# A 480-byte tile at the right end of on-chip memory in a fused window-attention and two-layer MoE kernel

## The chip, the cores and the metric

The kernel runs on one core of a Trainium2 chip (trn2). The metric is device microseconds of one execution, lower is better. Engines: PE is TensorE (matmuls; PEld its weight loads), DVE is VectorE, ACT is ScalarE, POOL is GpSimd, SP is SyncE, which issues the DMAs.

## The reference

Three blocks follow one another, all in float32, on 1536 tokens of width 512.

```
x = window_attention(q, k, v)           # (2, 8, 768, 64): 16-wide window, plus 24 block summaries
x = relu(x @ w_in) ** 2 @ w_out         # 512 -> 2048 -> 512; weights come as float64
rms = sqrt(mean(x * x, -1) + 1e-6); xn = x / rms * rms_g
g = xn @ w_gate; val = xn @ w_val       # 512 -> 1536
out = (silu(g) * val) @ w_out2          # 1536 -> 512
```

## The kernel before

**Work and order.** Attention runs over 12 groups of 128 tokens (`group`, `ptrans`, `av`) with plain float32 matmuls; its results go, split in a high and a low part, into `xhi`/`xlo`. Weights arrive as float64 words, are turned to float32 (`conv_a`, `conv_b`) and split in a high and a low part of type float32r (`split`, lines 195 and 196), which together fill one 4096-byte slot, the tile that `wslot` hands out. A product of the MoE layers is three float32r matmuls: high by high, high by low, low by high (`mm3`, line 509; `ff_out`, line 530). The first layer's `wi0` to `wi3` and `wo0` to `wo3` run between the attention groups, on halves of 256 columns. After attention everything is done in rounds (`steps_of`): for a few units f, for each of the 3 chunks of 512 tokens, `product` with 12 matmuls of 512 columns and, two steps later, `ff_out` with 12 more. In `product` (tiles `h`, `g`, `v`) the weights are the operand that is loaded into the array, and the tokens stream; in `ff_out` (tiles `y`, `z`) the hidden values are loaded and the weights stream, 512 columns of 4 bytes, 2048 bytes of each partition. The program is put in order by the tile framework's scheduler.

**Where tiles lie.** Every partition of on-chip memory is filled from both ends. Pools on the left hold `ident`, the raw and converted weights (`wpool`, 14 slots at 20,480 + 4096 n bytes), `xhi`/`xlo`, the hidden values `hhi`/`hlo` (their last tile ends at byte 174,080) and most partial sums `yp`. Pools with `side="right"` are laid downwards from byte 229,344, which is 32 more than a multiple of 64. During attention that is `ap`: `kT`, `vx`, `ksum`, `qT`, `t`, `vm`, `pT` and four 32-byte tiles `mx`, `sm`. When attention is over, `ap` is closed and `w2pool` takes its place: 9 more weight slots, at 192,480 + 4096 n bytes, and `grow`, `yp10`, `yp11`. Sizes on the right are multiples of 64 bytes, but for `mx` and `sm` (32 each), so nearly every tile there starts 32 bytes past a multiple of 64; every weight slot on the left starts at a multiple of 64.

**Which weights lie where.** Once `w2pool` is open, `wslot` counts the converted units: of each 18 the first 9 go to the right, the next 9 to the left.

```
k = side["n"] % (NRIGHT + NW - RAWS)     # 9 + 14 - 5 = 18
side["n"] += 1
if k < NRIGHT:
    return side["pool"].tile([P, 2, DM], F32R, tag="w2", name=name, bufs=NRIGHT)
```

In the order in which units are converted (`order`), this gives:

| side | units |
|---|---|
| left | wi0-4, wo0-3 (before `w2pool`); wi10-14, wo8-11; wg2-4, wv2, wv3, wp0-3; wg8-10, wv8-10, wp6-8 |
| right | wi5-9, wi15; wo4-7, wo12-15; wg0, wg1, wg5-7, wg11; wv0, wv1, wv4-7, wv11; wp4, wp5, wp9-11 |

Right are 32 units, all of them used on 512 columns, each by 12 matmuls for each of 3 chunks.

Of the kernel before, what the change touches and what calls it, by code (L numbers as in the profile page):

```python
# [10 lines left out]
F32 = mybir.dt.float32  # L11
# [21 lines left out]
def tile_window_attention_moe_moe2(  # L33
# [16 lines left out]
    P = 128  # L50
# [33 lines left out]
    psY = ctx.enter_context(tc.tile_pool(name="psY", bufs=MT // 2, space=PSUM))  # L84
    psB = ctx.enter_context(tc.tile_pool(name="psB", bufs=1, space=PSUM))

    ident = cpool.tile([P, P], F32, name="ident")
    make_identity(nc, ident)
    um = cpool.tile([P, KW + QT], F32, name="um")
# [55 lines left out]
    side = {"n": 0, "pool": None}  # L145
# [713 lines left out]
```

## Time and profile before

| | |
|---|---|
| three runs | 680.22, 681.25 (median), 683.86 us |
| profiled execution | span 681.0 us from the first to the last instruction; no other time is given for it |
| PE busy | 654.7 us (96%), 3644 matmuls |
| DVE / ACT / POOL busy | 404.4 / 305.8 / 4.1 us |
| moved by DMA | 54.22 MB, mean 80 GB/s |

The profiled span lies 0.25 us below the median of the runs. Busy shares are means over stages that have different limits: attention with its many short steps takes the first 160 us or so, and the MoE layers the rest. The chain of waits follows the work that ended last back from the end; where it shows one engine with no wait between its pieces, the time of that stretch is the sum of that engine's instructions. A piece of the chain "x12" is 12 instructions of one line, and its length runs to the start of the next piece, so its length by 12 is what one instruction costs the stretch. The mean duration of one matmul in the grouped view is longer than that, since matmuls overlap.

### The profile page before, as it was taken

Reading aid. Unit: us, or ns where it says so; the run is one execution under the profiler, and the core shown is the slowest. Engines: PE = TensorE matmul, PEld = TensorE weight load, DVE = VectorE, ACT = ScalarE, POOL = GpSimd, SP = SyncE. Lnnn points to the kernel's source line nnn. Section 1 sums busy time; section 2 is a strip of 40 time slices with the busy share of each in tenths; the row PEclk is TensorE's granted clock in tenths of the full one; section 3 lists DMA queues with packets and bytes.
Section 4 is the critical chain, followed back from the end, with each engine's and each line's share of the span. In section 5 each row is a group of like instructions: output and inputs, shape, how many; then the busy total and the mean of one; then the engine's idle time right before and its main releaser. Section 6 shows DMA issues by size and latency. Waiting matters only on the chain.

```text
span 681.0 us, 9361 instructions
## 1 busy us (share of the span) xinstructions
PE 654.7 (96%) x3644; PEld 533.9 (78%) x3644; DVE 404.4 (59%) x733; ACT 305.8 (45%) x637; POOL 4.1 (1%) x25
## 2 busy tenths in 40 slices
PE   7768998999999999999999999999999999999997
PEld 5456957888888888888888888888888888888885
DVE  4799758656999579726574795189613171313132
ACT  4597558365866447326352773167411131111110
POOL 2000000000000000000000000000000000000000
PEclk9769998999999999999999999999999999999999
DMA  9678556222522223001021251015300000001011
GB/s 244 147 247 190 131 171 160 68 49 91 189 62 94 93 63 123 31 1 62 13 98 46 68 180 62 1 34 162 113 1 1 0 1 0 1 1 62 1 62 63
DMA packets 78188, 54.22 MB, mean 80 GB/s; under 512 B 46080, under 2 KB 72704, under 8 KB 78144
## 3 DMA queue, kind: packets, MB, share of 16 engines
q1 hardware_dynamic: 78144, 53.62, 26.7%
q8 instruction: 29, 0.48, 0.3%
q14 instruction: 15, 0.12, 0.1%
HBM read 50.07 MB, written 3.15 MB: 78 GB/s over the span
## 4 chain that ended last, share of the span: by engine, by line
PE 86%; SPq 5%; DVE 4%; DMA 2%; ACT 1%; issue 1%; DVEq 0%; ACTq 0%
PE y L530 19%; PE h L509 18%; PE g L509 15%; PE v L509 15%; PE z L530 14%; SPq L404 3%; PE xps L488 1%; PE pps L467 1%; PE s L418 1%; SPq L303 1%; DMA raw_wo<-in_moe_w_out_dram 1%; PE xps L500 1%; ACT t L447 1%; SPq L292 1%; DMA raw_wi<-in_moe_w_in_dram 1%
## 5 line engine op out<-in xcount | busy, mean ns | idle before, releaser
L509 PE MATMUL h<-xhi,w_wi 128*128 128x512 f32 (+1 forms) x480 | 136.6, 357 | 1.8 <-ACT xhi L478 1.2
L530 PE MATMUL y<-w_wo,hhi 128*128 128x512 f32 x384 | 120.7, 398 | 1.9 <-ACT hhi L520 1.7
L805 DVE TENSOR_TENSOR sg<-v,sg 128x512 f32<-128x512 f32 x36 | 24.9, 692 | 134.8 <-PE v L509 134.8
L509 PEld LDWEIGHTS h<-xhi,w_wi 128*128 128x128 f32 x480 | 87.3, 195 | 15.7 <-ACT xhi L478 1.9
L509 PE MATMUL v<-xhi,w_wv 128*128 128x512 f32 x288 | 95.6, 393 | 0.0
L509 PE MATMUL g<-xhi,w_wg 128*128 128x512 f32 x288 | 95.4, 393 | 0.0
L530 PE MATMUL z<-w_wp,hhiz 128*128 128x512 f32 x288 | 89.0, 392 | 0.0
L509 PE MATMUL h<-xlo,w_wi 128*128 128x512 f32 (+1 forms) x240 | 86.1, 359 | 1.8 <-DVE xlo L479 1.8
L530 PEld LDWEIGHTS y<-w_wo,hhi 128*128 128x128 f32 x384 | 72.4, 190 | 18.2 <-ACT hhi L520 1.9
L530 PE MATMUL y<-w_wo,hlo 128*128 128x512 f32 x192 | 75.1, 401 | 0.0
L803 ACT ACTIVATE sg<-g 128x512 f32<-128x512 f32 x36 | 21.6, 600 | 104.6 <-PE g L509 102.4
L509 PEld LDWEIGHTS v<-xhi,w_wv 128*128 128x128 f32 x288 | 54.0, 188 | 12.3
L509 PEld LDWEIGHTS g<-xhi,w_wg 128*128 128x128 f32 x288 | 54.0, 188 | 12.3
L530 PEld LDWEIGHTS z<-w_wp,hhiz 128*128 128x128 f32 x288 | 54.0, 188 | 11.9
L657 ACT ACTIVATE r<-h 128x512 f32<-128x512 f32 x48 | 28.7, 598 | 71.3 <-PE h L509 71.2
L509 PE MATMUL g<-xlo,w_wg 128*128 128x512 f32 x144 | 56.6, 393 | 0.0
L509 PE MATMUL v<-xlo,w_wv 128*128 128x512 f32 x144 | 56.5, 393 | 0.0
L530 PE MATMUL z<-w_wp,hloz 128*128 128x512 f32 x144 | 55.9, 392 | 0.0
L509 PEld LDWEIGHTS h<-xlo,w_wi 128*128 128x128 f32 x240 | 46.9, 195 | 9.0 <-DVE xlo L479 2.4
L658 DVE TENSOR_TENSOR r<-h,r 128x512 f32<-128x512 f32 x48 | 33.0, 687 | 35.0 <-ACT r L657 35.0
L520 ACT CAST hhiz<-sg 128x512 fp32r<-128x512 f32 x36 | 22.4, 621 | 69.7 <-DVE sg L805 69.4
L530 PEld LDWEIGHTS y<-w_wo,hlo 128*128 128x128 f32 x192 | 36.2, 191 | 8.1 <-issue 0.2
(125 smaller groups left out, 897.5 us busy)
## 6 DMA issues: line engine op xcount, KB each, us to landing
raw_wi<-in_moe_w_in_dram SPq DMA_DIRECT2D x16, 512.0 KB
raw_wo<-in_moe_w_out_dram SPq DMA_DIRECT2D x16, 512.0 KB
raw_wg<-in_moe_w_gate_dram SPq DMA_DIRECT2D x12, 512.0 KB
raw_wv<-in_moe_w_val_dram SPq DMA_DIRECT2D x12, 512.0 KB
raw_wp<-in_moe_w_out_dram SPq DMA_DIRECT2D x12, 512.0 KB
kr<-in_k_dram SPq DMA_DIRECT2D x12, 256.0 KB
qr<-in_q_dram SPq DMA_DIRECT2D x12, 256.0 KB
vr<-in_v_dram SPq DMA_DIRECT2D x6, 512.0 KB
```

The costliest lines, as they stand in the source:

```text
L292: nc.sync.dma_start(t.rearrange("p h e d -> p h (e d)"), src[b, :, 2 * P * c : 2 * P * (c + 1), :].rearrange("h (p e) d -> p h (e d)", e=2),)
L303: nc.sync.dma_start(t[:, j].rearrange("p (h d) -> p h d", h=H), src[b, :, o : o + P, :].rearrange("h p d -> p h d"),)
L404: nc.sync.dma_start(vx[j : j + n, i0 + u], v[b, :, o : o + n, :].rearrange("h s d -> s h d"))
L418: mark[("s", g)] = nc.tensor.matmul(sl[e][QT * u : QT * u + QT, p, :], qT[rr, p, QT * u : QT * u + QT], kT[rr, p, o : o + NK], start=True, ...
L447: mark[("exp", g)] = nc.scalar.activation(t[:, h], t[:, h], AF.Exp, bias=mx[:, h : h + 1], accum_out=sm[:, h : h + 1])
L509: nc.tensor.matmul(ps, a_, b_, start=(i == 0), stop=(i == tot - 1))
L520: nc.scalar.copy(hi[:, 0:n], s[:, 0:n])
L530: nc.tensor.matmul(y, a_[:, ms], b_, start=(first and i == 0), stop=(last and i == 2))
L657: nc.scalar.activation(t, ps, AF.Relu)
L658: nc.vector.tensor_tensor(t, ps, t, op=ALU.mult)
L803: nc.scalar.activation(t, psg, AF.Silu)
L805: nc.vector.tensor_tensor(t, psv, t, op=ALU.mult)
```

## The change

A pool `lpool` is opened on the right before any other pool there, and one tile of 120 float32 values for each partition, 480 bytes, is placed in it. Nothing writes or reads the tile. All pools opened later on the right lie 480 bytes lower: their top is byte 228,864 = 64 x 3576, the weight slots of `w2pool` lie at 192,000 + 4096 n, and every tile there starts at a multiple of 64 except two of the 32-byte tiles `mx`, `sm`. Tiles on the left stay where they were. No instruction, wait or DMA is added, taken away or moved on any engine. Line numbers after this place grow by 2.

```
     psB = ctx.enter_context(tc.tile_pool(name="psB", bufs=1, space=PSUM))
 
+    lpool = ctx.enter_context(tc.tile_pool(name="lpool", bufs=1, side="right"))
+    lpool.tile([P, 120], F32, name="edge")
     ident = cpool.tile([P, P], F32, name="ident")
```

## Rows read from the trace of the kernel before

**Rows 1.** The page: the span, busy time by engine, PE in 40 slices

```profile
span 681.0 us, 9361 instructions
...
PE 654.7 (96%) x3644; PEld 533.9 (78%) x3644; DVE 404.4 (59%) x733; ACT 305.8 (45%) x637; POOL 4.1 (1%) x25
...
PE   7768998999999999999999999999999999999997
```

**Rows 2.** Busy time in stretches: from:to, length, engines (instructions), clock, DMA share, GB/s

```profile
23.10:29.90 6.80, 4.34 (x24) 4.04 (x26) 4.99 (x13) 4.01 (x7) 0.00 (x0) 0.50 0.51 103
40.20:50.30 10.10, 6.84 (x32) 6.04 (x31) 9.68 (x20) 8.57 (x26) 0.00 (x0) 0.50 0.64 155
67.50:70.80 3.30, 3.30 (x17) 3.20 (x16) 3.30 (x5) 1.01 (x1) 0.00 (x0) 0.50 0.83 251
115.30:122.00 6.70, 6.70 (x54) 5.66 (x55) 4.97 (x9) 5.33 (x20) 0.00 (x0) 0.50 0.45 141
150.00:676.00 526.00, 525.54 (x2389) 429.38 (x2389) 294.10 (x534) 210.89 (x373) 0.00 (x0) 1.00 0.17 56
```

**Rows 3.** What PE waited for, whole span: us, times, longest

```profile
PE qps L364 <- DMA qr<-in_q_dram: 7.6, 2, 4.9
...
PE y L530 <- ACT hhi L520: 1.7, 1, 1.7
...
PE y L530 <- ACT w_wo L195: 0.2, 1, 0.2
```

**Rows 4.** The chain that ended last, one round of the second layer: start, us, piece

```profile
471.72 2.73 PE g L509 x12
474.45 2.79 PE v L509 x12
477.24 2.73 PE z L530 x12
479.97 2.80 PE g L509 x12
482.77 2.79 PE v L509 x12
485.56 2.73 PE z L530 x12
...
493.88 2.80 PE z L530 x12
```

**Rows 5.** The same chain: two pieces of 18 matmuls of `y`, first layer

```profile
186.00 4.20 PE y L530 x18
...
285.86 4.08 PE y L530 x18
```

**Rows 6.** The same chain: left weights right behind right ones, then left alone

```profile
571.86 2.75 PE g L509 x12
574.60 2.72 PE v L509 x12
577.32 2.72 PE z L530 x12
```

**Rows 7.** Instructions by line and shape: the casts into slots, and two attention matmuls

```profile
L488 PE MATMUL xps<-pT,vx 120*64 120x64 f32 x384 | 17.7, 234 | 0.1
L418 PE MATMUL s<-kT,qT 64*64 64x120 f32 x384 | 17.6, 278 | 0.0
...
L195 ACT CAST w_wo<-x_wo 128x512 fp32r<-128x512 f32 x16 | 9.9, 620 | 3.2 <-DVE x_wo L189 2.5 <-PE y L530 0.6
...
L195 ACT CAST w_wp<-x_wp 128x512 fp32r<-128x512 f32 x12 | 7.4, 618 | 3.2 <-PE v L509 2.0 <-PE z L530 0.7 <-DVE x_wp L189 0.6
```

**Rows 8.** Busy time in the stretch right after attention, columns as in rows 2

```profile
165.00:205.00 40.00, 40.00 (x186) 32.98 (x186) 39.01 (x75) 27.75 (x50) 0.00 (x0) 1.00 0.44 144
```

**Rows 9.** The whole chain's shares of the span, by line

```profile
by line: PE y L530 19.2%; PE h L509 18.2%; PE g L509 14.6%; PE v L509 14.6%; PE z L530 14.4%; SPq L404 2.8%; PE xps L488 1.4%; PE pps L467 1.2%; PE s L418 1.1%; SPq L303 1.0%; DMA raw_wo<-in_moe_w_out_dram 1.0%; PE xps L500 0.8%; ACT t L447
```

## The prediction

> **What bounds the kernel now.** I first read the page: PE is busy for 654.7 of 681.0 us, and the slices show it at 9 tenths from the eighth slice on [rows 1]. Then the stretches: between 150 and 676 us PE is busy for 525.54 of 526.00 us at a granted clock of 1.00, which is the 2.4 GHz level [rows 2], while its waits for the other engines' results in the MoE layers are small: 1.7 us for ACT's high part of a hidden tile, 0.2 us for a converted weight [rows 3]. So from 150 us on only the pace of the matmuls counts. Before that the kernel is a mixture of short waits (7.6 us for `qr` alone [rows 3]) and of four stretches at half the clock [rows 2]. The whole chain says the same by line: the five rows of lines 509 and 530 hold 81% of the span, and attention's PE rows for `xps` and `s` 1.4% and 1.1% [rows 9].
>
> The change moves no instruction, so the question is whether a matmul or another instruction cares where its tile begins. The kernel before answers part of that itself, because the same matmul is run on weights in left slots (a start at a multiple of 64) and in right slots (32 past one). In one round of the second layer [rows 4] the pieces of 12 matmuls are, by the list of units: `g` on wg4 (left) 2.73 us, `v` on wv4 (right) 2.79, `z` on wp2 (left) 2.73, wg5 and wv5 (right) 2.80 and 2.79, wp3 (left) 2.73, and, two pieces further on, wp4 (right) 2.80. The side decides, not the line: `z` takes 2.73 on wp2 and wp3 and 2.80 on wp4, and `g` takes 2.73 on wg4 and 2.80 on wg5. That holds whether the weights stream (`z`) or are loaded (`g`, `v`). The first layer agrees: 18 matmuls of `y` on right slots (wo4, wo5) take 4.20 us, 18 on left slots (wo10, wo11) 4.08 [rows 5]. Per matmul this is 4.20/18 = 233.3 ns against 4.08/18 = 226.7 ns: 6.67 ns more. At 2.4 GHz that is 16 cycles, and 16 columns of 4 bytes are 64 bytes, which looks like one more piece of 64 bytes to be fetched when a row that is itself whole pieces starts in the middle of one.
>
> **The sum.**
> - *The right-slot matmuls.* 32 units x 3 chunks x 12 matmuls = 1152, each 6.67 ns shorter: -7.7 us. All lie in the stretch where PE has no gaps, so all of it is on the path. This is the term that carries the forecast.
> - *Left pieces behind right ones.* A piece with loaded left weights that follows a right piece takes 2.75 us instead of 2.72 [rows 6] (there wg8 behind wp5, then wv8 and wp6 at 2.72). The chain has 19 such whole pieces at 2.75: 19 x 0.03 = -0.6 us. The pieces of 2.79 (last matmul at the left pace already) and of 2.73 (last one at the right pace) about cancel each other.
> - *Attention's matmuls.* `vx`, `kT`, `qT`, `t` and `pT` move as well. No row shows such a float32 matmul with its tile at another start, so I bound it. At the one end nothing: a loss I exclude, since `vx`, `qT` and `pT` come to the start that is the faster one in [rows 5], and the windows of `kT`, which begin at steps of 304 bytes, only exchange one set of starts for another when all move by 480. At the other end each of the 384 + 384 instructions of `xps` and `s` [rows 7] saves the same 6.67 ns; two always run side by side, so 768 x 6.67 / 2 = 2.6 us. I take -0.3, near the lower end: half of the 768 work on `kT`, and an `xps` takes 234 ns for 64 columns [rows 7] where the big ones advance by 512 in 226.7, so one more piece has more time to come in beside it.
> - *VectorE and ScalarE.* They write the slots and read the tiles on the right. The casts into slots take 620 ns for `w_wo`, 8 of whose 16 units are right, and 618 ns for `w_wp`, 5 of 12 [rows 7]. A cost per right slot would pull the first above the second by 8/16 - 5/12 = 8% of it; a difference of 2 ns bounds it to about 25 ns a cast, on engines that wait for PE in the MoE layers. I put it at nothing; the cover is PE's unbroken work.
> - *DMAs.* 72 loads and 12 copies write `vx`. `vx` does not stand among PE's waits. I put them at nothing; what hides them is the work that PE does while `vx` is filled.
> - *What is late next.* Right after attention DVE is busy for 39.01 of 40 us [rows 8], since it converts the next weights there. If a faster PE had to wait for it, at most the gain of that stretch would be lost, about 9 right pieces x 0.08 = 0.7 us. Elsewhere nothing is close: between 150 and 676 us DVE is busy for 294 of 526 us [rows 2].
>
> Sum: -7.7 - 0.6 - 0.3 = -8.6 us, from the execution's 681.0 to 672.4 us. That execution lies 0.25 us below the median of the runs, so against the median of 681.25 I forecast 672.7 us, 1.3% faster.
>
> **A rule that speaks against it.** The rows show that 32 bytes past a multiple of 64 is a slow start for a right slot, or that the right side is slow whatever its start. The Trainium skill, in "SBUF — State Buffer", section "Specifications (TRN2)", gives cachelines of 16 bytes as the unit whose crossing costs something. Both 32 and 0 are multiples of 16, so by that rule the two starts touch equally many lines and the sum would be 0, a time of 681.25 us; the rows' step of 64 bytes' worth of columns does not fit it.
>
> **The rivals.**
> - *A: the side costs, not the start.* The right side could be slower because of where it lies (its addresses, or what it shares), and then moving it by 480 bytes changes nothing: 681.25 us. For it: before the change no right slot starts at a multiple of 64, so the trace cannot part the two. Against it: the hidden tiles that are loaded for the left `y` and `z` pieces reach up to byte 174,080 and go at 2.72 us, and the lowest right slot at 192,480 (wi5, wv4, wg11, wo12) is as slow as the highest, so a border would have to fall in just that gap; and a far address gives no reason for 16 cycles. Beside this stands the Trainium skill's rule of 16-byte lines, above, which would lead here.
> - *B: slower, through the clock.* In the first 150 us the clock falls to 0.50 (1.2 GHz) in four stretches, 3.3 to 10.1 us long and 26.9 us in all [rows 2]. A shift of attention's short waits could add one, if idle time of PE grows around the loads of `qr`. Price: a stretch like the longest, on work that PE bounds, costs 10.1/2 = 5 us; with A that gives 686 us. It decides the sign only if the gain in the MoE layers fails as well, or if over 17 us are added at half the clock. Against it: no instruction there changes its place or its number.
> - *C: only part.* PE gets its gain and gives 3 to 5 us of it back, by such a stretch of clock or by waits for conversions: 677 us. Against it: PE's gaps between 150 and 676 us sum to 0.46 us [rows 2], so the others keep up with it by a margin.
>
> **How the numbers follow.** Forecast 0.88, A 0.07, C 0.03, B 0.02. About 0.5%, 3.4 us, is what a measurement of this kernel can tell from no change; C's 677 lies beyond that. So faster 0.91, same 0.07, slower 0.02. The predicted time is the forecast's, 672.7. Its range: down by the rest of attention's bound (2.3 us, of which I take 1.7, since part of it lies beside other work), to 671.0; up by the terms that could fail (0.7 of DVE, 0.6 of the pieces behind right ones, 0.8 of attention and its DMAs) and by 1.2 us for the scatter of the runs, whose highest lay 2.6 above their median: 676.0. That holds nearly all of the forecast's 0.88, and needs no part of A.
>
> **What would show it.** Right: in the chain of the new profile every whole piece of 12 on line 511 (509 before) and on line 532 (530 before) takes 2.72 us, the same for units of both sides; 2.75 and 2.80 are gone; the stretch from the end of attention to the last matmul is some 8 us shorter, with PE busy throughout and DVE's and ACT's means as before. Wrong: pieces of 2.80 stay on right units (A); another stretch at clock 0.50 before 150 us (B); PE waits on `w_wi` or `w_wo` around 165 to 205 us (C).

## The result and the profile after

The changed kernel takes 674.5 us (median of 4 runs, 673.34 to 675.57), the one before 680.74 us (4 runs, 680.16 to 683.86): a ratio of 0.9899 with a 95% interval of 0.9868 to 0.9931, so it is faster by 0.7 to 1.3%. The forecast was 672.7 us, with a range of 671.0 to 676.0. The profiled execution of the changed kernel has a span of 673.9 us, against 681.0 before: 7.1 us less. With it comes its own time, 675.57 us, 1.7 us more than the span; in all executions on record a time is 1.7 to 1.9 us more than its span, so the sum is best compared span with span.

The chain of waits after, for the same stretch of the second layer as [rows 4]: start, length and piece.

```profile
468.19 2.72 PE g L511 x12
470.92 2.72 PE v L511 x12
473.63 2.72 PE z L532 x12
476.36 2.72 PE g L511 x12
479.07 2.72 PE v L511 x12
481.80 2.72 PE z L532 x12
...
489.95 2.72 PE z L532 x12
```

These are wg4, wv4, wp2, wg5, wv5, wp3 and wp4. Before, wv4, wg5, wv5 and wp4 stood at 2.79 or 2.80 and the left ones at 2.73; now no side can be told from the other.

To separate this from attention, the view by tile gives the last attention matmul (`xps`, last start) and the last matmul of all (`z`, last start). Before:

```profile
L488 PE MATMUL xps<-pT,vx x384: 222/222/368, 31.5 to 160.6; 120*64 120x64 f32 x192
...
L530 PE MATMUL z<-w_wp,hloz x144: 389/395/397, 393.8 to 676.2; 128*128 128x512 f32 x144
```

After:

```profile
L490 PE MATMUL xps<-pT,vx x384: 221/222/368, 32.6 to 161.5; 120*64 120x64 f32 x192
...
L532 PE MATMUL z<-w_wp,hloz x144: 388/390/398, 390.8 to 669.1; 128*128 128x512 f32 x144
```

From the end of attention to the last matmul it took 676.2 - 160.6 = 515.6 us, and takes 669.1 - 161.5 = 507.6 us: 8.0 us less. Attention itself ends 0.9 us later. The median duration of these `z` matmuls (the middle number) falls from 395 to 390 ns.

The stretches after, with the columns of [rows 2]:

```profile
24.80:31.60 6.80, 5.50 (x43) 5.20 (x44) 3.21 (x10) 3.42 (x7) 0.00 (x0) 0.50 0.48 91
41.80:52.10 10.30, 7.25 (x33) 6.85 (x33) 9.90 (x21) 8.78 (x25) 0.00 (x0) 0.50 0.63 142
113.50:123.80 10.30, 10.30 (x75) 8.47 (x75) 7.01 (x11) 6.75 (x22) 0.00 (x0) 0.50 0.48 137
150.00:669.00 519.00, 518.53 (x2397) 430.67 (x2396) 294.46 (x534) 211.16 (x375) 0.00 (x0) 1.00 0.17 56
165.00:205.00 40.00, 40.00 (x194) 33.76 (x193) 39.59 (x77) 28.42 (x51) 0.00 (x0) 1.00 0.45 145
```

Three stretches at half the clock in place of four, of about the same sum (27 us). From 150 us on PE has gaps of 0.47 us, as before. In the 40 us right after attention DVE is fuller still, 39.59 us [rows 8], and PE 40.00.

The instructions by line and shape that answer to [rows 7]:

```profile
L420 PE MATMUL s<-kT,qT 64*64 64x120 f32 x384 | 18.9, 291 | 0.0
L490 PE MATMUL xps<-pT,vx 120*64 120x64 f32 x384 | 17.7, 234 | 0.0
...
L197 ACT CAST w_wo<-x_wo 128x512 fp32r<-128x512 f32 x16 | 9.9, 620 | 3.2 <-DVE x_wo L191 2.7 <-PE y L532 0.5
...
L197 ACT CAST w_wp<-x_wp 128x512 fp32r<-128x512 f32 x12 | 7.4, 617 | 3.1 <-PE v L511 1.8 <-PE z L532 0.7 <-DVE x_wp L191 0.6
```

The casts and attention's `xps` take what they took. Attention's `s` is busy for 18.9 us instead of 17.6, but the median of one is 263 ns in both traces; the half-clock stretches lie at other places.

### The profile page after: what moved, and what is told of

It is laid out like the page before. It is cut to its first block, busy times and chain, and to the rows that moved or that the text cites. A ratio compares the mean times of both kernels' runs of the same rounds, so it can differ in the third digit from the quotient of the medians.

```text
span 673.9 us, 9361 instructions
## 1 busy us (share of the span) xinstructions
PE 646.7 (96%) x3644; PEld 534.0 (79%) x3644; DVE 403.7 (60%) x733; ACT 305.2 (45%) x637; POOL 4.0 (1%) x25
## 4 chain that ended last, share of the span: by engine, by line
PE 88%; SPq 4%; DVE 2%; DMA 2%; ACT 2%; issue 1%; DVEq 0%; ACTq 0%
PE y L532 19%; PE h L511 19%; PE v L511 15%; PE g L511 15%; PE z L532 14%; SPq L406 2%; PE xps L490 2%; PE s L420 2%; DMA raw_wi<-in_moe_w_in_dram 1%; PE pps L469 1%; SPq L305 1%; ACT t L449 1%; PE xps L502 1%; PE qps L366 1%; SPq L294 1%
## 5 line engine op out<-in xcount | busy, mean ns | idle before, releaser
L511 PE MATMUL h<-xhi,w_wi 128*128 128x512 f32 (+1 forms) x480 | 134.8, 354 | 2.5 <-ACT w_wi L197 1.7
```

Source lines behind the costliest of these rows:

```text
L511: nc.tensor.matmul(ps, a_, b_, start=(i == 0), stop=(i == tot - 1))
```

## The experiments

The first question was rival A: start or place. The second arose from the first answer: if the start counts, then why. "Mod 512" is what is left of a start address when whole multiples of 512 are taken off. "Stage" is the time from the last `xps` to the last matmul, from the rows by tile of each profile; it leaves out what attention's clock does.

| run | start of right slots (mod 512) | start of left operands (mod 512) | stage, us | ratio to before, 95% interval |
|---|---|---|---|---|
| before | 480 | 0 | 515.6 | |
| changed | 0 | 0 | 507.6 | 0.9899 (0.9868 to 0.9931) |
| e1_edge32 | 448 | 0 | 513.5 | 0.9986 (0.9961 to 1.0012) |
| e2_edge512 | 480 | 0 | 515.6 | 1.0002 (0.9981 to 1.0023) |
| e7_edge992 | 0 | 0 | 507.6 | 0.9861 (0.9793 to 0.9929) |
| e8_left480 | 480 | 480 | 507.6 | 0.9898 (0.9833 to 0.9962) |
| e5_left32 | 0 | 32 | 515.6 | one run |
| e10_edge224 | 256 | 0 | 507.6 | 0.9883 (0.9845 to 0.9921) |

**Start or place: 32 and 512 bytes.**

```
-    lpool.tile([P, 120], F32, name="edge")
+    lpool.tile([P, 8], F32, name="edge")       # e1_edge32
+    lpool.tile([P, 128], F32, name="edge")     # e2_edge512
```

> The tile at the right end is 32 bytes instead of 480, so everything on the right moves by 32 bytes only and starts at a multiple of 64, at addresses 32 below those of the kernel before. Theory (the start counts): as the changed kernel, about 674 us, and every piece of 12 matmuls with 512 columns at 2.72 us. Rival (the place on the right counts, and moving down by 480 took the tiles out of it): as the kernel before, about 681 us, with pieces of 2.80 on the right units.

> The tile at the right end is 512 bytes, so everything on the right lies 32 bytes lower than in the changed kernel and starts 32 past a multiple of 64 again. Theory (the start counts): as the kernel before, about 681 us, pieces of 2.80 us on the right units and 2.72 on the left ones. Rival (the place counts): as the changed kernel, about 674 us, all pieces at 2.72.

With 512 bytes, 32 below the changed kernel, the gain is gone: 681.13 us, a stage of 515.6 us. So 32 bytes up or down decide, not the region, and rival A falls. But with 32 bytes, where every tile starts at a multiple of 64 as well, the median is 680.02 us, no faster than before by its interval. The stage says what happened. The chain of e1_edge32:

```profile
465.58 2.72 PE g L511 x12
468.30 2.75 PE v L511 x12
471.05 2.72 PE z L532 x12
473.77 2.75 PE g L511 x12
...
487.48 2.80 PE z L532 x12
490.28 2.80 PE g L511 x12
```

`z` on wp4 (the piece at 487.48) still takes 2.80, that is, a streamed right slot at a multiple of 64 still costs 6.67 ns a matmul; loaded ones (wv4, wg5) cost 2.75, or 2.80 right behind a slow piece (wg7). A multiple of 64 is neither the condition nor enough. My theory and its rival are both wrong here.

**Other distances in one kernel.** The slot is made longer, and each unit starts at another place in it.

```
-                return side["pool"].tile([P, 2, DM], F32R, tag="w2", name=name, bufs=NRIGHT)
+                t = side["pool"].tile([P, 2 * DM + 16], F32R, tag="w2", name=name, bufs=NRIGHT)
+                o = (1, 0, 4, 12, 15, 8, 2, 6, 14)[k]
+                return t[:, o : o + 2 * DM].rearrange("p (e f) -> p e f", e=2)
```

> The changed kernel, but each right weight slot is 64 bytes longer and its unit starts at 4, 0, 16, 48, 60, 32, 8, 24 or 56 bytes into it, by its number among the right ones: four units (wi6, wi15, wg5, wv11) stay at 0, the other 28 lie off a multiple of 64. Theory (one more piece of 64 bytes, whatever the distance): every unit off 0 takes 2.80 us for 12 matmuls, those at 0 take 2.72; 28 x 36 x 6.67 ns = 6.7 us above the changed kernel, about 681 us. Rival 1 (only crossing lines of 16 bytes costs): 16, 32 and 48 at 2.72, the others slower. Rival 2 (the cost grows with the distance from 64): pieces between 2.72 and 2.80 in steps.

One execution took 680.24 us, with a stage of 514.5 us, near what "any distance costs" gives. But the units at 0 past a multiple of 64 were not fast (these slots, 4160 bytes apart, begin at different places within 512 bytes), and one at 16 past a multiple of 64 was:

```profile
472.75 2.80 PE v L513 x12
...
478.28 2.75 PE g L513 x12
481.03 2.72 PE v L513 x12
```

The `v` at 472.75 is wv4 (4 past a multiple of 64), the `g` at 478.28 wg5 (a multiple of 64, at 448 within 512), the `v` at 481.03 wv5 (16 past one, at 400 within 512). The slowest was a streamed unit, wo12 at 452 within 512: 2.86 us for 12 (the piece at 290.97), more than the 2.80 that one more piece of 64 bytes would give. None of the three theories fits that.

**Shorter rows.** In the kernel before, the streamed rows of `ff_out` are cut from 512 to 504 columns.

```
+                n = DM if first and i == 0 else DM - 8
                 nc.tensor.matmul(
-                    y, a_[:, ms], b_, start=(first and i == 0), stop=(last and i == 2)
+                    y[:, 0:n], a_[:, ms], b_[:, 0:n], start=(first and i == 0), stop=(last and i == 2)
                 )
```

> The kernel before (right slots 32 past a multiple of 64), but in the second product of both layers the streamed rows are 504 columns long, 2016 bytes, except in the first matmul of each sum: the last 8 columns get that one term alone. 2016 bytes touch 32 pieces of 64 bytes from a start at 0 and from a start at 32 alike. Theory (pieces are counted): pieces of 12 matmuls of y and z that stream from right slots are as fast as those from left slots, 2.68 to 2.72 us both, while h, g and v, where the weights are loaded, keep 2.80 against 2.72. Rival (a start at 32 costs 16 cycles whatever the length): y and z at 2.76 from the right and 2.68 from the left.

```profile
472.60 2.72 PE z L531 x12
475.32 2.80 PE g L509 x12
478.12 2.80 PE v L509 x12
480.92 2.72 PE z L531 x12
...
489.24 2.78 PE z L531 x12
...
497.62 2.76 PE z L531 x12
```

One execution took 678.03 us. Left units (wp2, wp3, at 472.60 and 480.92) are no faster for 8 columns less: 2.72, not 2.68, so here the number of columns alone does not set the pace; no run shows what does. Right ones take 2.76 (wp5, at 497.62), as the rival says, and 2.78 where the first matmul of every sum is a full one (wp4, at 489.24). They are not as fast as the left ones, which speaks against the theory, but the step is 0.04 us for 12 and not the rival's 0.08. Neither holds as a whole, and this run does not decide.

**Own start or start against each other.** In e7_edge992 the tile has 248 values, 992 bytes. In the other two runs a tile lies on the left, below the weight pool, on top of the kernel before (e8) and of the changed one (e5).

```
+    bpool = ctx.enter_context(tc.tile_pool(name="bpool", bufs=1))
+    bpool.tile([P, 120], F32, name="base")     # e8_left480; [P, 8] in e5_left32
     wpool = ctx.enter_context(tc.tile_pool(name="wpool", bufs=1))
```

> The tile at the right end is 992 bytes: the right side lies 512 bytes lower than in the changed kernel, and its weight slots start at a multiple of 512 again (not only of 64, as in the run with 32 bytes). Theory (what counts is the start within 512 bytes): all pieces of 12 at 2.72 us, a profiled span of about 674 us, some 7 us below the kernel before. Rival (the changed kernel lies at one lucky place): pieces of 2.75 to 2.80 us on right units and about 681 us.

> The kernel before, with the right side left where it was (its slots start at 480 past a multiple of 512), and a tile of 480 bytes put on the left below the weight pool, so that the left slots, the tokens and the hidden values start at 480 past a multiple of 512 too. Theory P (what counts is how the loaded and the streamed operand stand to each other): all pieces at 2.72 us, about 674 us, as the changed kernel, though no operand starts at a multiple of 64. Theory Q (each operand pays for its own start): all 2592 float32r matmuls pay, most of them for both operands; pieces of 2.80 to 2.88 us everywhere, 690 us or more.

> The changed kernel, with a tile of 32 bytes on the left below the weight pool: left weights, tokens and hidden values start at 32 past a multiple of 512, the right weights at 0. Theory P (the two operands' starts against each other): left units 2.72 us for 12 matmuls, as both operands lie at 32; right units 2.80; about 681 us. Theory Q (each pays for its own start): no piece at 2.72; right units 2.80, left units 2.80 or, if the two costs add, 2.88; about 690 to 700 us.

e8_left480 is the run that settles it. The right side stays as it was in the kernel before, 32 past a multiple of 64, and everything that meets it on PE is moved to the same distance. Now no float32r matmul has an operand at a multiple of 64, and all are fast: 674.75 us against 682.08 for the kernel before, a stage of 507.6 us. Its chain:

```profile
469.25 2.72 PE g L511 x12
471.97 2.72 PE v L511 x12
474.69 2.72 PE z L532 x12
...
491.01 2.72 PE z L532 x12
```

The `v` at 471.97 (wv4) and the `z` at 491.01 (wp4) are right units, the other two left ones.

e5_left32 is the counter-test: right slots where the change puts them, the left moved by 32 bytes. The whole gain is lost (a stage of 515.6 us), and in the chain the right units are the slow ones, though it is they that start at a multiple of 512:

```profile
472.88 2.73 PE g L513 x12
475.61 2.79 PE v L513 x12
478.40 2.73 PE z L534 x12
481.13 2.80 PE g L513 x12
...
495.04 2.80 PE z L534 x12
```

So theory P holds against Q: what costs is the distance between the starts of the loaded and of the streamed operand. Neither pays for its own start. Which two meet can be read in the trace of the kernel before, from the start of one matmul to the start of the next (the stretch of [rows 4]): the first eleven of wg4 (left) take 226 or 227 ns, the last, with wv4 (right) to be loaded next, 235; those of wv4 take 230 to 235, and the last, with a left operand next, 226. It is the streamed operand of one matmul against the loaded one of the matmul behind it. e7_edge992 gives the changed kernel's stage at another place: 671.88 us against 682.08.

**Which distances.** The slots 512 bytes longer, units at multiples of 64 (and 16, 32), then at finer steps; and the right side as a whole at 256.

```
+                t = side["pool"].tile([P, 2 * DM + 128], F32R, tag="w2", name=name, bufs=NRIGHT)
+                o = (64, 8, 16, 32, 48, 80, 96, 4, 112)[k]       # e6_scan
+                o = (36, 100, 28, 40, 20, 44, 52, 34, 60)[k]     # e9_scan2
```

> The changed kernel, but each right weight slot is 512 bytes longer and its unit starts at 256, 32, 64, 128, 192, 320, 384, 16 or 448 bytes past a multiple of 512, by its number among the right ones; tokens and hidden values stay at 0. Theory (period 512): every right unit is slower than 2.72 us for 12 matmuls, 2.80 for streamed weights and 2.74 to 2.80 for loaded ones; about 680 us. Rival (period 128 or 256): units at 256, or at 128, 256 and 384, take 2.72 like those at 0.

> The tile at the right end is 224 bytes, so that the right slots start at 256 past a multiple of 512, all other operands at a multiple of 512. Theory (the loaded and the streamed operand must start at the same place within 256 bytes): all pieces of 12 at 2.72 us; from the last attention matmul to the last of all 507.6 us, as in the changed kernel. Rival (within 512 bytes; that the units at 256 were fast was the luck of their neighbours): right pieces at 2.75 to 2.80 and up to 515.6 us.

> As the scan before, with the right units at 144, 400, 112, 160, 80, 176, 208, 136 and 240 past a multiple of 512. Theory in its plain form (any other distance within 256 bytes costs): no right piece at 2.72 us. Rival (the two reads meet only at some distances, and a loaded operand some 144 bytes off misses the streamed one): loaded units at 144 and 400 at 2.72 us, as the one unit at 400 in the first scan, streamed ones at 144 slow.

e6_scan and e9_scan2 were executed once each, 679.6 and 679.81 us. The chain of e6_scan: units at 256 (wv4, at 472.13), 32 (wg5), 64 (wv5), then 128 and 192 (wg6, wv6), 320 (wp4).

```profile
472.13 2.72 PE v L513 x12
474.85 2.73 PE z L534 x12
477.58 2.79 PE g L513 x12
480.37 2.80 PE v L513 x12
483.17 2.76 PE z L534 x12
485.92 2.79 PE g L513 x12
488.72 2.79 PE v L513 x12
491.51 2.75 PE z L534 x12
```

At 256 a loaded unit is as fast as at 0, and so is a streamed one (wo12, in the first layer, 2.73 with the next unit's first load in it). e10_edge224 confirms it for all right slots at once: stage 507.6 us, 672.6 us. The period is thus 256 bytes; 128 and 64 are not free. In e9_scan2 one more distance is fast in places:

```profile
291.48 2.80 PE y L534 x12
294.28 2.80 PE h L513 x12
297.08 2.77 PE y L534 x12
...
472.85 2.72 PE v L513 x12
...
478.29 2.73 PE g L513 x12
481.01 2.80 PE v L513 x12
483.81 2.77 PE z L534 x12
486.57 2.80 PE g L513 x12
```

Loaded units at 144 (wv4, at 472.85) and at 400 = 256 + 144 (wg5, at 478.29) take 2.72 and 2.73, while a streamed unit at 144 (`y` on wo12, at 291.48) takes 2.80, and units at 112 and 160 (wv5, at 481.01, and wg6, at 486.57) take 2.80. So "any other distance costs" is too plain. But the rival's reason, that two reads 144 bytes apart miss each other, does not hold either: another loaded unit at 400 (wi15, at 294.28), right behind the slow wo12, takes 2.80. And a streamed unit at 112, where the loaded operand also lies 144 bytes further on within 256, takes 2.77 (wo13, at 297.08), and behind a fast piece 2.76 (wp9, from start to start). At a distance of 144 the pace thus depends on the piece before and on which operand is the weight. At a distance of 0 it comes back: the left wp3 at 483.81 takes 2.77 behind a slow unit, but its ninth to eleventh matmuls are at 226 to 227 ns again. e1_edge32 shows the same dependence on the piece before, with 2.75 and 2.80 for loaded units at one and the same distance.

## Why the prediction was right, and where its reason was not

- *What bounds the kernel:* right. From 150 us on PE has no gaps before or after, and the 8.0 us of the stage go through to the end: the span fell by 7.1, with attention ending 0.9 us later.
- *The right-slot matmuls (-7.7 us) and the left pieces behind right ones (-0.6):* 8.3 us forecast, 8.0 measured for the stage. From start to start, the matmuls of the right units lost 7.35 us and those of the left ones 0.63. The pieces of 2.75, 2.79 and 2.80 are gone from the round shown, and the price of 6.67 ns read from [rows 5] was right within 5% (7.35 us over 1152 matmuls is 6.4 ns), as it came from the same instructions in the same kernel.
- *The reason given for that price is wrong.* I put it that one more piece of 64 bytes has to be fetched when a row starts in the middle of one. e1_edge32 starts every right row at a multiple of 64 and still pays; e8_left480 starts none there and does not pay. In its place the runs show a cost of the distance between the two operands' starts, with a period of 256 bytes. The trace of before could not tell the two apart, since there the left operands were all at 0 and the right ones all at 480 within 512. The size was right because the 480 bytes of this change happen to bring that distance to 0, and that was luck: with 32 bytes, which by my reason are as good, I would have forecast a gain some 6 us too large.
- *Attention's matmuls (-0.3 of 0 to 2.6 us):* mis-sized; the lower end was right. `xps` takes 17.7 us for 384, 234 ns each, before and after, and the median of `s` stays at 263 ns. The reason is another than the ones I weighed: `vx` and `pT`, and `kT` and `qT`, all lie on the right and move together, so the distance between their starts is the same before and after. The last attention matmul starts 0.9 us later, with the half-clock stretches at other places.
- *VectorE, ScalarE, DMAs at nothing:* right as far as a row shows: the casts took 620 and 618 ns, and take 620 and 617. *DVE late next:* did not happen; PE stays at 40.00 of 40 us there.
- *Against the median:* I took the profiled execution to lie 0.25 us below the median of the runs. A span is 1.7 us shorter than its execution's time, so that one lay at about 682.7, some 1.4 us above the median. The forecast itself, the median less 8.6 us, does not hang on this. The medians fell by 6.2 us (680.74 to 674.5), less than the stage's 8.0; with 4 runs each, 673.34 to 675.57 and 680.16 to 683.86, the rest is not taken apart.
- *Rival A* is refuted by e2_edge512, e7_edge992 and e8_left480, *C* by the stage. *B* did not come. But attention's end varies between 155.4 us (e1_edge32) and 162.5 us (e8_left480) in the profiles taken, nearly as much as the gain, and it goes with the time at half the clock before it: 17 us in the first of these, and some 27 us in the kernel before, the changed one, e5, e8, e9 and e10, which all end at 160.1 us or later. Those 10 us more would cost 5 us where PE bounds the work, and the ends lie 4.7 to 7.1 us apart; that the clock is the cause fits, but no run changes it by itself. The profiled execution of e1_edge32 had a span of 673.7 us, like the changed kernel's, on an end of attention 6.1 us earlier, while its stage was 513.5 us and the median of its ten runs 680.02 us.
- *The rule weighed:* by the 16-byte cachelines of the Trainium skill, "SBUF — State Buffer", section "Specifications (TRN2)", neither this change nor e8_left480 should do anything, and both gain about 1%: the measurement decides. None of these matmuls reads with a stride, so what the page says of hits for each line is not tested by them.

What stays open is why: that both reads meet in something that repeats every 256 bytes fits all runs, but no run here shows it, nor why a distance of 144 keeps a fast pace for loaded weights and not for streamed ones.

## What to carry to other kernels

Where float32r matmuls run without gaps, compare the start addresses of the operand that is loaded and of the one that is streamed: here a difference of 0 within 256 bytes gave 226.7 ns for 512 columns; the others gave mostly up to 233.3, 3% more, in one case 238 (2.86 us for 12), and 144 gave the fast and the slow pace. Rounding all tiles to 64 bytes is not enough, and moving either side is as good as moving the other, so one unused tile of the right size does it. And if the same matmul runs at two paces within one kernel, sort its instances by where their operands lie before anything else; then change one address at a time, since one layout cannot part an operand's own start from its distance to the other.

## What was not expected of the hardware

- Operands both 480 past a multiple of 512 run at full pace (e8_left480, 2.72 us for 12), and an operand at a multiple of 512 is slow if its partner lies 32 off (e5_left32, 2.80).
- A streamed row of 504 columns takes as long as one of 512: 2.72 us for 12 from left slots (e4_504).
- At one and the same distance the pace can depend on the piece before: a loaded unit at 400 takes 2.73 behind a fast piece and 2.80 behind a slow one (e9_scan2).
- Whether plain float32 matmuls pay for a distance is not shown: both operands of attention's `xps` (234 ns before and after) moved together.
